# A routed feed-forward kernel: eight widths instead of three for each expert's step, and a last block of at most 64 tokens computed in strips of the TensorE array

## Chip, cores and metric

One core of one Trainium2 chip. The metric is device time in microseconds; the kernel before takes 586.5 us, the median of three runs.

## The reference

An attention layer over 4 batches, 8 heads, 768 positions and 64 dimensions (local window of 96, 8 global keys) gives 3072 token rows of 512. Each token goes to one of 8 experts, the one with the largest logit, and its row is

```
h = np.maximum(np.einsum('ecd,edf->ecf', disp, w1), 0.0)   # 512 -> 1024
y = np.einsum('ecf,efd->ecd', h, w2)                       # 1024 -> 512
out[i] = gate_w[i] * y[expert_idx[i], pos[i]]
```

With the inputs as drawn the eight experts get 455, 416, 361, 397, 367, 410, 395 and 271 tokens.

## The kernel before

The first 240 us compute attention and route the tokens; the change does not touch their code. Then the experts follow one after the other, e = 0 to 7. Their tokens stand in up to four blocks of 128 slots (`T4` = 512 slots). Layer 1 has the weights stationary and the tokens moving: for each of 8 slices f of the hidden layer, 12 matmuls (`layer1`, L844) of w columns into one PSUM bank, `h_ps[f % 2]`, where w is the width of the step. Layer 2 has a block of 128 tokens stationary and 512 columns of w2 moving: 3 matmuls (`layer2`, L852 to L854) for each f and block into the block's bank `y_ps[a]`. Both layers work in float32r on numbers split into a high and a low part, so that a product is three matmuls. `hidden` (L871, L872) makes the two parts of the hidden slice, hh on ScalarE (ACT) and hl on VectorE (DVE); four "pieces" for every second f split the raw weights in the same way (L142 on ACT, L143 on DVE), and `turn` brings in the next expert's tokens (L325 on TensorE, L762, L765).

In step f TensorE runs layer 2 of slice f - 2 for the blocks that every expert has (`SURE`, three of them), then a test of the register `arms[e]` chooses one of three copies of the rest (`widths`): layer 1 with w = 512, 448 or 384, and behind it layer 2 for the fourth block where w is over 384. Only TensorE branches. Slices 6 and 7 of layer 2 run in `last`, behind the next expert's first layer 1, with the fourth block under a test that has no other arm (`with_last`, L830); `finish` (L775) scales a block by the gate and POOL scatters its rows (L777).

The order on TensorE, ACT and DVE in this stage is the order in which the code is written; DMA issues on SP and POOL are placed by the scheduler. Raw weights come in tiles `wr`, eight buffers of 256 KB, two tiles for w1 and two for w2 of a step of two slices; the first three steps are loaded during attention.

Of the kernel before, what the change touches and what calls it, by code (L numbers as in the profile page):

```python
# [20 lines left out]
P = 128  # L21
# [6 lines left out]
def fused(ctx: ExitStack, tc, q, k, v, wg, w1, w2, out, n_global, n_local, cap):  # L28
# [93 lines left out]
    def raw_weights(step, pool, name, bufs, after=()):  # L122
# [662 lines left out]
    STEP, LEAST = 64, 6  # L785
    NV = T4 // STEP - LEAST + 1
    SURE = FIXED - 1
    arm = moe.tile([P, E], I32, name="arm", bufs=1)

    def fill_levels():  # L790
        few = moe.tile([P, E], F32, name="few", bufs=1)
        nc.vector.tensor_scalar(few, run, float(min(cap, T4)), float(STEP - 1), op0=ALU.min, op1=ALU.add)
        nc.vector.tensor_copy(arm, few)
        nc.vector.tensor_scalar(arm, arm, STEP.bit_length() - 1, None, op0=ALU.logical_shift_right)
        nc.vector.tensor_scalar(arm, arm, LEAST, LEAST, op0=ALU.max, op1=ALU.subtract)

    nblk = rt.tile([1, E + 2], I32, name="nblk", bufs=1)
# [15 lines left out]

    arms = {}
# [4 lines left out]
    def widths(e):  # L819

        with tc.If(arms[e] > 0) as more:
            with tc.If(arms[e] > 1) as most:
                yield T4
            with most.Else():
                yield T4 - STEP
        with more.Else():
            yield STEP * LEAST

    def with_last(e):
        with tc.If(arms[e] > 0):  # L830
            yield


    h_ps = [bankB([P, T4]) for _ in range(FP)]
    y_ps = [bankA([P, DM]) for _ in range(FIXED)]

# [28 lines left out]
    def hidden(hs, f, s):  # L865

        if f not in hs:
            hs[f] = (moe.tile([P, T4], F32R, name="hh", bufs=5), moe.tile([P, T4], F32R, name="hl", bufs=5))
        h = h_ps[f % 2]
        hh, hl = hs[f]  # L870
# [35 lines left out]
    for e in range(E):  # L906
# [6 lines left out]
        for f in range(NF):  # L913
# [11 lines left out]
            if f == 4 and e + 1 < E:  # L925
                load_arm(e + 1)
# [125 lines left out]
```

## Time and profile before

| | |
|---|---|
| median of three runs | 586.5 us (584.51 to 587.95) |
| the profiled execution's own time | 591.38 us |
| its span, first to last instruction | 589.2 us |
| TensorE busy | 552.0 us, 94% of the span |
| DVE, ACT, POOL busy | 320.6, 300.6, 107.6 us |
| mean granted TensorE clock | 0.965 of full |

The profile is one execution. Busy time is the time in which at least one matmul was under way, and matmuls overlap, so the time that one costs is the distance from its start to the next one's start. Times in rows count from the span's start.

### The profile page before, as it was taken

To read this page: it belongs to the slowest core of one execution; us is meant where nothing else is said; L and a number is where in the kernel's file an instruction comes from. 1 tells how busy PE (TensorE), PEld (TensorE's weight loads), DVE (VectorE), ACT (ScalarE), POOL (GpSimd) and SP (SyncE) were. 2 spreads that over 40 slices of the span, in tenths; PEclk is the share of its full clock that TensorE was granted. 3 is DMA by queue.
4 is the path that set the end of the run, shared out by engine and by line. 5 is a ranking of instruction groups with operands and counts; after the bars stand their busy time and mean duration, and the time that the engine had idled before them with its cause. 6 is when DMAs were issued, how large, how long until landed. Compare 5 with 4: busy or idle time off the path is not lost.

```text
span 589.2 us, 10890 instructions
## 1 busy us (share of the span) xinstructions
PE 552.0 (94%) x3725; PEld 455.2 (77%) x3725; DVE 320.6 (54%) x1037; ACT 300.6 (51%) x798; POOL 107.6 (18%) x183
## 2 busy tenths in 40 slices
PE   8999987979799999889999999999999999999990
PEld 5677775857677777778888889888898888888970
DVE  6788885858577976624434445343453433533510
ACT  4886775757577785223344354533544434434320
POOL 5103020300103032223122122211222112002011
PEclk9999997979789999799999999999999999999996
DMA  9855554656565422067443455345455453333000
GB/s 214 212 146 146 146 126 153 155 126 160 121 174 130 118 57 82 20 138 264 156 156 126 143 169 179 132 152 159 136 175 169 136 157 123 120 103 129 2 21 24
DMA packets 119262, 78.90 MB, mean 134 GB/s; under 512 B 85837, under 2 KB 102221, under 8 KB 119184
## 3 DMA queue, kind: packets, MB, share of 16 engines
q1 hardware_dynamic: 112608, 63.10, 38.2%
q0 software_dynamic: 5888, 14.71, 8.1%
q8 instruction: 46, 0.75, 0.6%
q14 instruction: 32, 0.26, 0.2%
q10 hardware_dynamic: 688, 0.07, 0.1%
HBM read 60.87 MB, written 14.75 MB: 128 GB/s over the span
## 4 chain that ended last, share of the span: by engine, by line
issue 47%; PE 30%; POOL 10%; DMA 6%; ACT 3%; DVE 1%; POOLq 1%; SPq 0%; DVEq 0%; ACTq 0%
PE bankA L514 8%; POOL out_dram L777 5%; POOL xg L336 5%; DMA nat_v<-in_moe_w_dram 5%; PE bankB L548 4%; PE bankC L458 4%; PE bankC L574 3%; PE bankC L577 3%; PE bankB L555 3%; ACT sc L530 2%; PE bankC L169 2%; PE bankA L190 1%; DMA table<-pay,slot_of 1%; PE bankA L200 1%; PE bankB L74 1%
## 5 line engine op out<-in xcount | busy, mean ns | idle before, releaser
L872 DVE SCALAR_TENSOR_TENSOR hl<-bankB,hh 128x512 fp32r<-128x512 f32 (+1 forms) x67 | 44.6, 668 | 180.6 <-ACT hh L871 180.4
L871 ACT ACTIVATE hh<-bankB 128x512 fp32r<-128x512 f32 (+1 forms) x67 | 38.8, 579 | 172.3 <-PE bankA L854 100.9
L530 ACT ACTIVATE sc<-sc,mx 128x232 f32<-128x232 f32 (+1 forms) x192 | 89.1, 466 | 29.2 <-DVE mx L521 27.8
L844 PE MATMUL bankB<-xh,w1h 128*128 128x448 f32 (+3 forms) x268 | 95.1, 357 | 3.3 <-ACT xh L762 2.1
L844 PE MATMUL bankB<-xh,w1l 128*128 128x448 f32 (+3 forms) x268 | 94.1, 353 | 0.0
L852 PE MATMUL bankA<-w2h,hh 128*128 128x512 f32 x232 | 93.8, 404 | 0.0
L854 PE MATMUL bankA<-w2h,hl 128*128 128x512 f32 x232 | 91.6, 395 | 1.5 <-DVE hl L872 1.5
L853 PE MATMUL bankA<-w2l,hh 128*128 128x512 f32 x232 | 90.8, 391 | 0.0
L521 DVE CUSTOM_DVE_ANT_0 sc<-bankA,bias 128x232 f32<-128x232 f32 (+1 forms) x192 | 64.7, 377 | 17.4 <-PE bankA L514 16.6
L844 PE MATMUL bankB<-xl,w1h 128*128 128x448 f32 (+3 forms) x268 | 61.5, 353 | 0.0
L844 PEld LDWEIGHTS bankB<-xh,w1h 128*128 128x128 f32 x268 | 51.5, 192 | 9.1 <-ACT xh L762 2.7
L844 PEld LDWEIGHTS bankB<-xh,w1l 128*128 128x128 f32 x268 | 51.6, 193 | 4.7
L336 POOL DMA_INDIRECT xg<-xrows,gi x28 | 28.8, 1028 | 135.1 <-PE bankC L325 123.2
L854 PEld LDWEIGHTS bankA<-w2h,hl 128*128 128x128 f32 x232 | 43.6, 188 | 12.2 <-DVE hl L872 2.3
L777 POOL DMA_INDIRECT out_dram<-ysb,tb x30 | 29.6, 986 | 121.0 <-ACT ysb L775 120.1
L844 PEld LDWEIGHTS bankB<-xl,w1h 128*128 128x128 f32 x268 | 48.8, 192 | 2.8
L852 PEld LDWEIGHTS bankA<-w2h,hh 128*128 128x128 f32 x232 | 43.7, 188 | 7.1 <-ACT hh L871 0.4
L853 PEld LDWEIGHTS bankA<-w2l,hh 128*128 128x128 f32 x232 | 43.7, 188 | 7.1
L514 PE MATMUL bankA<-KH,QH 64*128 64x232 f32 (+1 forms) x192 | 41.9, 352 | 6.8 <-ACT QH L459 5.9
L548 PE MATMUL bankB<-ident,sc 128*128 128x128 f32 x192 | 41.1, 297 | 4.3 <-ACT sc L530 4.3
L514 PEld LDWEIGHTS bankA<-KH,QH 64*128 64x128 f32 x192 | 23.9, 191 | 22.0 <-issue 7.9
L577 PE MATMUL bankC<-ptB,nat_v 128*64 128x128 f32 x384 | 38.7, 281 | 0.0
(154 smaller groups left out, 958.8 us busy)
## 6 DMA issues: line engine op xcount, KB each, us to landing
wr<-in_moe_w_dram SPq DMA_DIRECT2D x116, 256.0 KB
nat_q<-in_q_dram SPq DMA_DIRECT2D x24, 256.0 KB
nat_k<-in_k_dram SPq DMA_DIRECT2D x24, 256.0 KB
nat_v<-in_v_dram SPq DMA_DIRECT2D x24, 256.0 KB
xrows<-xr SPq DMA_DIRECT2D x23, 256.0 KB
v<-nat_v SPq DMA_DIRECT2D x20, 192.0 KB
nat_v<-in_moe_w_dram SPq DMA_DIRECT2D x12, 256.0 KB
out_dram<-ysb,tb POOLq DMA_INDIRECT x30, 2.8
```

What stands on the lines that cost most here:

```text
L336: ld = nc.gpsimd.indirect_dma_start(out=xg, out_offset=None, in_=xrows[0:n], in_offset=bass.IndirectOffsetOnAxis(ap=gi.bitcast(U32), axis= ...
L514: m = nc.tensor.matmul(pss[hh][:, gg, :], qq[rows, g, :], win, start=a == 0, stop=a == 2)
L521: nc.vector.tensor_tensor_reduce(out=sc[:, a, 0:w], in0=pss[hh][:, gg, :], in1=bias[:, 2 * g + hh, :], scale=1.0, scalar=3.0e38, op0=ALU.a ...
L530: un["e"] = nc.scalar.activation(sc[:, a, 0:w], sc[:, a, 0:w], AF.Exp, bias=un["mx"][:, a:a + 1], scale=-1.0, accum_out=sm[:, a:a + 1])
L548: un["turned"] = nc.tensor.transpose(pb[:, a, :], un["sc"][:, a, o:o + P], ident)
L577: nc.tensor.matmul(o_ap, d["v"][:, h * D:(h + 1) * D], un["ptB"][:, a, :], start=j == 0, stop=True)
L777: w = nc.gpsimd.indirect_dma_start(out=out, out_offset=bass.IndirectOffsetOnAxis(ap=rows.bitcast(U32)[:, 0:1], axis=0), in_=ysb, in_offset ...
L844: nc.tensor.matmul(h_ps[:, s], ww[:, c, fs], xx[:, c, s], start=n == 0, stop=n == 3 * KC - 1)
L852: nc.tensor.matmul(y, hh[:, t], w2h[:, fi], start=f == 0, stop=False)
L853: nc.tensor.matmul(y, hh[:, t], w2l[:, fi], start=False, stop=False)
L854: nc.tensor.matmul(y, hl[:, t], w2h[:, fi], start=False, stop=f == NF - 1)
L872: nc.vector.scalar_tensor_tensor(hl[:, s], h[:, s], 0.0, hh.bitcast(F32)[:, s], op0=ALU.max, op1=ALU.subtract)
```

## The change

Widths now go in steps of 32 from 288 to 512, eight copies of a step, chosen by a tree of three tests. `SURE` falls to two blocks. In a copy of width w, layer 2 runs first: whole blocks as before (`whole`, a last block counts as whole if it has more than 64 tokens of the width), and a last block of 32 or 64 goes through `beside`: one plain float32 matmul for each f instead of three float32r ones, with 32 or 64 stationary columns, written to a strip of 32 or 64 partitions of the bank `y_ps[3]`; slices f, f + 1, ... go to different strips, so each strip holds a partial sum, and `finish` adds the strips with three DVE operations under a factor `gates` that is the gate or 0. `beside` runs for slices 0 to 3 in step 5 and for slices 4 to 7 in `last`. It needs the hidden slice and w2 unsplit: a third product `hr` of `hidden` (128x256, on ACT) and raw w2 tiles `w2r` (512 KB, seven buffers) that stay until `beside` has read them; `wr` keeps four buffers for w1. The raw w2 of the first three steps is loaded a second time. `take_beside` (15 small DVE operations, once) makes the gates and the row numbers; four small operations join `fill_levels`. In `last` the third and fourth block are now finished first, and slice 7 of the first two blocks comes behind them.

With the counts above the widths before are 512, 448, 384, 448, 384, 448, 448, 384; now 480, 416, 384, 416, 384, 416, 416, 288. Experts 1, 3, 5, 6 have three whole blocks and a strip of 32 instead of four blocks, expert 7 two blocks and a strip of 32 instead of three; experts 0, 2 and 4 keep their blocks and have no strip.

```diff
--- before.py
+++ after.py
...
@@ -128,9 +128,11 @@
             parts = {}
             m = shape[1] // 2
+            if keep and n == "w2":
+                parts["r"] = keep(shape)
             for i in range(2):
                 s = slice(i * m, (i + 1) * m)
-                r = pool.tile([P, m, shape[2]], F32, name=name, bufs=bufs)
+                r = parts["r"][:, s] if "r" in parts else pool.tile([P, m, shape[2]], F32, name=name, bufs=bufs)
                 ld = nc.sync.dma_start(out=r, in_=src[:, s])
...
@@ -773,6 +775,12 @@
     def finish(e, a, rows, y):
         ysb = moe.tile([P, DM], F32, name="ysb", bufs=FIXED)
         nc.scalar.activation(ysb, y, AF.Copy, scale=rows[:, 1:2])
+        if a == FIXED - 1:
+
+            for n, o, m in ((1, 2 * GR, 2 * GR), (0, GR, GR), (0, 3 * GR, GR)):
+                nc.vector.scalar_tensor_tensor(ysb[0:m], y[o:o + m], gates[0:m, e, n:n + 1], ysb[0:m],
+                                               op0=ALU.mult, op1=ALU.add)
...
-    STEP, LEAST = 64, 6
-    NV = T4 // STEP - LEAST + 1
-    SURE = FIXED - 1
+    GR, FINE = 32, 32
+    LOW = 9
+    SURE = GR * LOW // P
...
+    FIRST_ARM = GR * (LOW - 1) // FINE + 1
+    NV = T4 // FINE - FIRST_ARM + 1
...
-    def widths(e):
-
-        with tc.If(arms[e] > 0) as more:
-            with tc.If(arms[e] > 1) as most:
-                yield T4
-            with most.Else():
-                yield T4 - STEP
-        with more.Else():
-            yield STEP * LEAST
-
-    def with_last(e):
-        with tc.If(arms[e] > 0):
-            yield
...
+    def widths(e):
+
+        def among(lo, hi):
+            if hi - lo == 1:
+                yield FINE * (lo + FIRST_ARM)
+                return
+            mid = (lo + hi) // 2
+            with tc.If(arms[e] > mid - 1) as more:
+                yield from among(mid, hi)
+            with more.Else():
+                yield from among(lo, mid)
+        yield from among(0, NV)
...
+    def beside(e, fs, w, hs):
+
+        y = y_ps[FIXED - 1]
+        a, rows = w // P, -(-(w % P) // GR) * GR
+        if rows in (GR, 2 * GR):
+            n = P // rows
+            for f in fs:
+                o = f % n * rows
+                hr = hs[f][2]
+                nc.tensor.matmul(y[o:o + rows], hr[:, (a - SURE) * P:(a - SURE) * P + rows],
+                                 wparts[e * (NF // FP) + f // FP][1]["r"][:, f % FP], start=f < n, stop=f >= NF - n)
+
+    def whole(w):
+
+        return range(SURE, w // P + (w % P > 2 * GR))
...
+    def plain(shape):
+        return moe.tile(shape, F32, name="w2r", bufs=7)
+
     def fetch(step, after=()):
         if step < STEPS and step not in wparts:
-            pieces[step] = raw_weights(step, moe, "wr", 8, after)
+            pieces[step] = raw_weights(step, moe, "wr", 4, after, plain)
...
         nc.scalar.activation(hh[:, s], h[:, s], AF.Relu)
         nc.vector.scalar_tensor_tensor(hl[:, s], h[:, s], 0.0, hh.bitcast(F32)[:, s], op0=ALU.max, op1=ALU.subtract)
+        if s.stop > SURE * P:
+            nc.scalar.activation(hr, h[:, SURE * P:], AF.Relu)
...
+    for step in range(PREFETCH):
+        t = wparts[step][1]["r"] = plain([P, FP, DM])
+        ld = nc.sync.dma_start(out=t, in_=w2[0, step * FP * P:(step + 1) * FP * P, :].rearrange("(f p) d -> p f d", p=P))
+        tc.add_manual_dep(ld.ins, got.ins.name, SYNC)
     fetch(PREFETCH, [got])
...
-            if f > 1:
-                for a in range(SURE):
-                    if e > 0 or f - 2 >= EARLY or a >= FIRST:
-                        second(f - 2, a)
+            h = h_ps[f % 2]
+
+            fs = (f - 2,) if f > 1 else ()
+            for a in range(SURE):
+                second([i for i in fs if e > 0 or i >= EARLY], a)
             part = slice(FIRST * P if e == 0 and f < EARLY else 0, T4)
             for w in widths(e) if e > 0 or f > 1 else ():
-                layer1(e, f, h_ps[f % 2], xh, xl, slice(part.start, w))
-                if f > 1 and w > SURE * P:
-                    second(f - 2, SURE)
+                for a in whole(w):
+                    second(fs, a)
+                if f == 5:
+                    beside(e, range(0, 4), w, hs)
+                layer1(e, f, h, xh, xl, slice(part.start, w))
             hidden(hs, f, part)
             if f == 0 and last is not None:
                 last()
+            if f == 3 and e == 0:
+                to = take_beside(tb)
...
-        def last(e=e, second=second):
+        def last(e=e, second=second, hs=hs):
             for a in range(SURE):
-                for f in (NF - 2, NF - 1):
-                    second(f, a)
+                second((NF - 2,), a)
+            for w in widths(e):
+                beside(e, range(4, NF), w, hs)
+                for a in whole(w):
+                    second((NF - 2, NF - 1), a)
+            rest = [finish(e, a, to[:, e, a - SURE], y_ps[a]) for a in range(SURE, FIXED)]
+            rest[0]()
+            for a in range(SURE):
+                second((NF - 1,), a)
                 finish(e, a, first["early"][:, a] if e == 0 and a < FIRST else tb[:, e, a], y_ps[a])()
-            for _ in with_last(e):
-                for f in (NF - 2, NF - 1):
-                    second(f, SURE)
-            finish(e, SURE, tb[:, e, SURE], y_ps[SURE])()
+            rest[1]()
...
```

On TensorE, step 5 of expert 1 before: the copy for w = 448 has layer 1 and then the fourth block, and a branch ends it (the rows from its last layer 1 group to the next copy; every row is an instruction, x4 four alike, and a plain matmul row holds its weight load).

```order
L844 MATMUL bankB<-xl,w1h 128x448 x4
L852 MATMUL bankA<-w2h,hh 128x512
L853 MATMUL bankA<-w2l,hh 128x512
L854 MATMUL bankA<-w2h,hl 128x512
L822 UNCONDITIONAL_BRANCH
```

And now, the copy for w = 416 in step 5 of expert 3:

```order
L884 MATMUL bankA<-w2h,hh 128x512
L885 MATMUL bankA<-w2l,hh 128x512
L886 MATMUL bankA<-w2h,hl 128x512
L897 MATMUL bankA<-w2r,hr 32x512 [waits DMAHW6_49]
L897 MATMUL bankA<-w2r,hr 32x512 [waits DMAHW7_49]
L897 MATMUL bankA<-w2r,hr 32x512 [waits DMAHW0_49]
L897 MATMUL bankA<-w2r,hr 32x512 [waits DMAHW1_49,Activation_49]
L876 MATMUL bankB<-xh,w1h 128x416
```

The three matmuls of L884 to L886 are the third block, which stood ahead of the tests before; the fourth block's three are gone, four strip matmuls stand between layer 2 and layer 1, and each of the four waits for a load of its own.

On TensorE, the test for the fourth block in `last` before (expert 1; the other experts' are alike):

```order
L830 COMPARE_AND_BRANCH
L852 MATMUL bankA<-w2h,hh 128x512
L853 MATMUL bankA<-w2l,hh 128x512
L854 MATMUL bankA<-w2h,hl 128x512
L852 MATMUL bankA<-w2h,hh 128x512
L853 MATMUL bankA<-w2l,hh 128x512
L854 MATMUL bankA<-w2h,hl 128x512
L830 UNCONDITIONAL_BRANCH
L830 UNCONDITIONAL_BRANCH [waits PE_49]
```

And now the lower copies of the tree that stands there, w = 320 and 288, to the end of the tree and the slice 7 of the first block behind it:

```order
L897 MATMUL bankA<-w2r,hr 64x512 [waits DMAHW2_49]
L897 MATMUL bankA<-w2r,hr 64x512 [waits DMAHW3_49,Activation_49]
L863 UNCONDITIONAL_BRANCH
L897 MATMUL bankA<-w2r,hr 32x512 [waits DMAHW7_49]
L897 MATMUL bankA<-w2r,hr 32x512
L897 MATMUL bankA<-w2r,hr 32x512 [waits DMAHW2_49]
L897 MATMUL bankA<-w2r,hr 32x512 [waits DMAHW3_49,Activation_49]
L863 UNCONDITIONAL_BRANCH
L884 MATMUL bankA<-w2h,hh 128x512
L885 MATMUL bankA<-w2l,hh 128x512
L886 MATMUL bankA<-w2h,hl 128x512 [waits DVE_49]
```

The path that skips the fourth block had a wait of TensorE for its own matmuls (PE_49); every path of the new tree holds matmuls, and no such wait stands in it.

On SP, the first loads of the expert stage before (tbf is an early copy of the table of slots, tb the table, wr raw weights of step 3 on):

```order
L174 DMA xrows<-xr_last 128x512 [waits DMAHW4_49,DVE_49]
L134 DMA wr<-in_moe_w_dram 128x2x256 [waits DMAHW1_49,DMAHW2_49,DMAHW0_49,DMAHW5_49,DMASW2_49,DMAHW6_49,PE_49,DMAHW7_49,Activation_49,Pool_49]
L738 DMA tb<-table 128x4x2 [waits DMASW7_49,DMASW3_49,DMASW0_49]
L738 DMA tb<-table 128x4x2 x4
L738 DMA tb<-table 128x4x2 [waits DMAHW3_49]
L738 DMA tb<-table 128x4x2 [waits DMAHW4_49]
L738 DMA tb<-table 128x4x2 [waits DMAHW5_49]
L134 DMA wr<-in_moe_w_dram 128x2x256 [waits DMAHW6_49]
L134 DMA wr<-in_moe_w_dram 128x512 [waits DMAHW7_49]
```

And now:

```order
L959 DMA w2r<-in_moe_w_dram 128x2x512 [waits DMAHW1_49,DMAHW2_49,DMAHW0_49,DMAHW5_49,DMASW2_49,DMAHW6_49,PE_49,DMAHW7_49,Activation_49,Pool_49]
L740 DMA tb<-table 128x4x2 [waits DMASW7_49,DMASW3_49,DMASW0_49]
L740 DMA tb<-table 128x4x2 x4
L740 DMA tb<-table 128x4x2 [waits DMAHW3_49]
L740 DMA tb<-table 128x4x2 [waits DMAHW4_49]
L740 DMA tb<-table 128x4x2 [waits DMAHW5_49]
L959 DMA w2r<-in_moe_w_dram 128x2x512 [waits DMAHW6_49]
L959 DMA w2r<-in_moe_w_dram 128x2x512 [waits DMAHW7_49]
L136 DMA wr<-in_moe_w_dram 128x2x256 [waits DMAHW0_49]
```

The three second loads of raw w2, 512 KB each, have moved in ahead of the first w1 tile of step 3.

## Rows read from the trace of the kernel before

**Rows 1.** The page's busy times (us, share of the span, instructions), granted TensorE clock in 40 slices of the span (tenths of full), and the queue that brings TensorE's instructions (packets, MB, share of 16 engines' time).

```profile
span 589.2 us, 10890 instructions
PE 552.0 (94%) x3725; PEld 455.2 (77%) x3725; DVE 320.6 (54%) x1037; ACT 300.6 (51%) x798; POOL 107.6 (18%) x183
...
PEclk9999997979789999799999999999999999999996
...
q8 instruction: 46, 0.75, 0.6%
```

**Rows 2.** Busy time of each engine in stretches of the expert stage (stretch, its length, busy us and instructions of TensorE matmuls, weight loads, DVE, ACT, POOL, then granted clock, DMA share, GB/s).

```profile
260.00:270.00 10.00, 8.54 (x39) 6.64 (x38) 3.98 (x8) 3.14 (x6) 5.17 (x5) 1.00 0.90 297
...
300.00:340.00 40.00, 40.00 (x196) 34.81 (x195) 18.69 (x37) 16.98 (x31) 6.07 (x6) 1.00 0.45 143
```

**Rows 3.** All waits of TensorE's matmuls from 260 us on (who, for whom: us in total, times, longest).

```profile
PE bankA L854 <- DVE hl L872: 1.5, 1, 1.5
PE bankB L844 <- PEq L830: 1.2, 2, 0.6
```

**Rows 4.** Groups of instructions by shape, 258 to 575 us (x count | busy us, mean ns of one | idle before and its releaser).

```profile
L844 PE MATMUL bankB<-xh,w1h 128*128 128x448 f32 x128 | 46.9, 366 | 1.2 <-PEq L830 1.2
...
L872 DVE SCALAR_TENSOR_TENSOR hl<-bankB,hh 128x512 fp32r<-128x512 f32 x61 | 42.2, 692 | 177.3 <-ACT hh L871 177.3
...
L871 ACT ACTIVATE hh<-bankB 128x512 fp32r<-128x512 f32 x61 | 36.5, 598 | 160.2 <-PE bankA L854 98.5 <-PE bankB L844 61.7
L142 ACT CAST w1h<-wr 128x512 fp32r<-128x512 f32 x58 | 32.9, 617 | 0.7 <-DMA wr<-in_moe_w_dram 0.7
...
L844 PE MATMUL bankB<-xh,w1h 128*128 128x384 f32 x96 | 32.4, 338 | 0.0
...
L775 ACT ACTIVATE ysb<-bankA,tb 128x512 f32<-128x512 f32 x30 | 20.3, 688 | 19.8 <-PE bankA L854 19.8
...
L871 ACT ACTIVATE hh<-bankB 128x256 fp32r<-128x256 f32 x2 | 0.8, 384 | 3.4 <-PE bankA L854 2.4 <-PE bankB L844 1.0
```

**Rows 5.** TensorE's matmuls in order of time (start us, us, instruction): the first of twelve layer 1 matmuls of 512, then 448 columns, the layer 2 matmul behind each twelve, and the next layer 1 twenty-four layer 2 matmuls later.

```profile
285.89 0.39 PE L844 MATMUL bankB<-xh,w1h 128*128 128x512 f32 x1
...
288.68 0.40 PE L852 MATMUL bankA<-w2h,hh 128*128 128x512 f32 x1
...
289.38 0.37 PE L844 MATMUL bankB<-xh,w1h 128*128 128x448 f32 x1
...
291.80 0.40 PE L852 MATMUL bankA<-w2h,hh 128*128 128x512 f32 x1
...
297.32 0.36 PE L844 MATMUL bankB<-xh,w1h 128*128 128x448 f32 x1
```

**Rows 6.** The same view, twelve layer 1 matmuls of 256 columns and of 384 columns, first and behind the last.

```profile
256.61 0.28 PE L844 MATMUL bankB<-xh,w1h 128*128 128x256 f32 x1
...
258.02 0.40 PE L852 MATMUL bankA<-w2h,hh 128*128 128x512 f32 x1
...
344.40 0.34 PE L844 MATMUL bankB<-xh,w1h 128*128 128x384 f32 x1
...
346.49 0.40 PE L852 MATMUL bankA<-w2h,hh 128*128 128x512 f32 x1
```

**Rows 7.** The same view in the attention stage. L190 is the router's product: four float32 matmuls of 32 stationary columns and 384 moving ones, each to its own 32 partitions; a float32 product leaves two records, so x8. L458 and L548 use all 128 columns. L577 has 64 stationary columns, two products beside each other in two halves, x4 for two products; a group like it (L574) stands between the two shown.

```profile
67.23 0.60 PE L458 MATMUL bankC<-ident,nat_q 128*128 128x128 f32 x4
67.76 0.85 PE L190 MATMUL bankA<-xt,wg_sb 128*32 128x384 f32 x8
68.54 0.33 PE L548 MATMUL bankB<-ident,sc 128*128 128x128 f32 x1
...
71.36 0.66 PE L458 MATMUL bankC<-ident,nat_k 128*128 128x128 f32 x4
71.85 0.60 PE L548 MATMUL bankB<-ident,sc 128*128 128x128 f32 x4
...
236.48 0.39 PE L577 MATMUL bankC<-ptB,nat_v 128*64 128x128 f32 x4
...
236.93 0.39 PE L577 MATMUL bankC<-ptB,nat_v 128*64 128x128 f32 x4
```

**Rows 8.** TensorE in order of time where expert 2 skips its fourth block.

```profile
375.45 0.40 PE L854 MATMUL bankA<-w2h,hl 128*128 128x512 f32 x1
376.43 0.48 PE L844 MATMUL bankB<-xh,w1h 128*128 128x448 f32 x1 [0.58 <-PEq L830]
```

**Rows 9.** The branches on L821 on TensorE's sequencer (duration ns min/median/max, first and last start): all of them, and the one between 340.5 and 341.5 us, which chooses the copy whose first matmul starts at 344.40 us.

```profile
L821 PEldq COMPARE_BRANCH  x62: 65/70/340, 257.7 to 563.3; - x62
...
L821 PEldq COMPARE_BRANCH  x1: 207/207/207, 340.8 to 340.8; - x1
```

**Rows 10.** ACT in expert 0, in order of time (idle before and its releaser in brackets).

```profile
262.59 0.62 ACT L142 CAST w1h<-wr 128x512 fp32r<-128x512 f32 x1 [0.71 <-DMA wr<-in_moe_w_dram]
266.92 0.60 ACT L871 ACTIVATE hh<-bankB 128x512 fp32r<-128x512 f32 x1 [3.70 <-PE bankA L854]
```

**Rows 11.** The end: ACT and POOL in order of time from the last layer 1 on.

```profile
569.22 0.60 ACT L871 ACTIVATE hh<-bankB 128x512 fp32r<-128x512 f32 x1 [3.57 <-PE bankB L844]
573.89 1.26 ACT L775 ACTIVATE ysb<-bankA,tb 128x512 f32<-128x512 f32 x2 [0.69 <-PE bankA L854]
...
576.13 0.97 POOL L777 DMA_INDIRECT out_dram<-ysb,tb  x1 [0.30 <-issue]
```

More of the change, by code (lines that the diff above doesn't have):

```diff
@@ L120, in fused, with raw_weights @@
     wparts = {}
-    def raw_weights(step, pool, name, bufs, after=()):
+    def raw_weights(step, pool, name, bufs, after=(), keep=None):
         e, fp = divmod(step, NF // FP)
@@ L781, in finish @@
         return scatter
-    STEP, LEAST = 64, 6
-    NV = T4 // STEP - LEAST + 1
-    SURE = FIXED - 1
+    GR, FINE = 32, 32
+    LOW = 9
+    SURE = GR * LOW // P
+    level = moe.tile([P, E], I32, name="level", bufs=1)
+    FIRST_ARM = GR * (LOW - 1) // FINE + 1
+    NV = T4 // FINE - FIRST_ARM + 1
     arm = moe.tile([P, E], I32, name="arm", bufs=1)
+    nblk = rt.tile([1, E + 2], I32, name="nblk", bufs=1)
     def fill_levels():
         few = moe.tile([P, E], F32, name="few", bufs=1)
[L792 to L797, printed above, removed]
+        for t, step, low in ((arm, FINE, FIRST_ARM), (level, GR, LOW)):
+            nc.vector.tensor_scalar(few, run, float(min(cap, T4)), float(step - 1), op0=ALU.min, op1=ALU.add)
+            nc.vector.tensor_copy(t, few)
+            nc.vector.tensor_scalar(t, t, step.bit_length() - 1, None, op0=ALU.logical_shift_right)
+            nc.vector.tensor_scalar(t, t, low, low, op0=ALU.max, op1=ALU.subtract)
     def count_blocks():
@@ L812, in count_blocks, with take_beside @@
         nc.vector.tensor_scalar(nblk, nblk, 7, None, op0=ALU.logical_shift_right)
+    gates = moe.tile([P, E, 2], F32, name="gates", bufs=1)
+    def take_beside(tb):
+        swap = moe.tile([P, E], F32, name="swap", bufs=1)
+        nc.vector.tensor_scalar(swap, level, 2.0, None, op0=ALU.is_lt)
+        to = moe.tile([P, E, 2, 2], F32, name="to", bufs=1)
+        for c, t in ((0, I32), (1, F32)):
+            d = moe.tile([P, E], t, name="d", bufs=2)
+            i, o = tb.bitcast(t)[:, :, :, c], to.bitcast(t)[:, :, :, c]
+            nc.vector.tensor_tensor(d, i[:, :, SURE], i[:, :, SURE + 1], op=ALU.subtract)
+            nc.vector.tensor_tensor(d, d, swap, op=ALU.mult)
+            nc.vector.tensor_tensor(o[:, :, 0], i[:, :, SURE], d, op=ALU.subtract)
+            nc.vector.tensor_tensor(o[:, :, 1], i[:, :, SURE + 1], d, op=ALU.add)
+        bits = moe.tile([P, E], I32, name="bits", bufs=1)
+        for n, m in ((0, P // GR - 1), (1, P // GR // 2)):
+            nc.vector.tensor_scalar(bits, level, m, None, op0=ALU.bitwise_and)
+            nc.vector.tensor_scalar(gates[:, :, n], bits, 0.0, None, op0=ALU.is_equal)
+            nc.vector.tensor_tensor(gates[:, :, n], gates[:, :, n], to[:, :, 1, 1], op=ALU.mult)
+        return to
     arms = {}
@@ L867, in hidden @@
         if f not in hs:
-            hs[f] = (moe.tile([P, T4], F32R, name="hh", bufs=5), moe.tile([P, T4], F32R, name="hl", bufs=5))
+            hs[f] = (moe.tile([P, T4], F32R, name="hh", bufs=5), moe.tile([P, T4], F32R, name="hl", bufs=5),
+                     moe.tile([P, T4 - SURE * P], F32, name="hr", bufs=7))
         h = h_ps[f % 2]
-        hh, hl = hs[f]
+        hh, hl, hr = hs[f]
         nc.scalar.activation(hh[:, s], h[:, s], AF.Relu)
         nc.vector.scalar_tensor_tensor(hl[:, s], h[:, s], 0.0, hh.bitcast(F32)[:, s], op0=ALU.max, op1=ALU.subtract)
+        if s.stop > SURE * P:
+            nc.scalar.activation(hr, h[:, SURE * P:], AF.Relu)
     EARLY = 3
@@ L897, in fused @@
                 xs[2](FIRST + a, y_ps[FIRST + a])
-            layer2(0, f - 2, a, y_ps[a], *hs0[f - 2])
+            layer2(0, f - 2, a, y_ps[a], *hs0[f - 2][0:2])
     for f in range(2):
@@ L908, in fused, with second @@
         hs = hs0 if e == 0 else {}
-        def second(f, a, e=e, hs=hs):
-            layer2(e, f, a, y_ps[a], *hs[f])
+        def second(fs, a, e=e, hs=hs):
+            for f in fs:
+                layer2(e, f, a, y_ps[a], *hs[f][0:2])
         for f in range(NF):
```

## Prediction

> **What bounds the kernel now.** I read the windows of the expert stage first, because the change touches nothing earlier. In the stretch 300 to 340 us TensorE's matmuls are busy 40.00 of 40.00 us at a granted clock of 1.00, while DVE has 18.7, ACT 17.0 and the DMA queues 45% [rows 2]. Next come the waits: from 260 us to the end all of TensorE's waits together are one of 1.5 us for DVE's hl and two of about 0.6 us for its own sequencer at L830 [rows 3]. So in these 300 us nothing but the number and the width of matmuls sets the time, until the tail, where the last expert's blocks go through ACT and POOL one behind the other [rows 11]. A matmul taken away from this stage is worth its spacing in the timeline, and a matmul added costs it. That spacing comes from rows 5 and 6.
>
> **A. Layer 2 matmuls removed.** Twenty-four layer 2 matmuls in a row take 297.32 - 291.80 = 5.52 us, 0.230 us each [rows 5]. Experts 1, 3, 5 and 6 lose their fourth block and expert 7 its third: 5 experts x 8 slices x 3 = 120 matmuls, -27.6 us.
>
> **B. Narrower layer 1.** Twelve matmuls take 2.79 us at 512 columns, 2.42 at 448 [rows 5], 2.09 at 384 and 1.41 at 256 [rows 6], so 0.2325, 0.2017, 0.1742 and 0.1175 us each. From 448 to 416 (experts 1, 3, 5, 6: 4 x 8 x 12 = 384 matmuls, of which the row of one of the three products counts 128 [rows 4]) half the step between the two rows is saved, 0.0138 us each: -5.3. From 384 to 288 (expert 7, 96 matmuls) 288 lies a quarter of the way from 256 to 384, at 0.1317, so 0.0425 each: -4.1. From 512 to 480 (expert 0, the six steps that choose a copy, 72 matmuls) 0.0154 each: -1.1. Together -10.5. The least that the narrower copies can save is nothing, if 416 costs what 448 does; but the four widths lie almost on one line, so I take the line.
>
> **C. The skipped test.** When experts 2 and 4 skip the fourth block, TensorE stands 0.58 to 0.6 us for its own earlier matmuls [rows 3, 8]. In the new tree every path has matmuls and no such wait: -1.2.
>
> **D. The strips.** Ten groups (two each for experts 1, 3, 5, 6, 7) of four float32 matmuls with 32 stationary and 512 moving columns. The nearest row is the router's product: four of them with 384 columns, eight records, in 68.54 - 67.76 = 0.78 us [rows 7], the change back to whole-array matmuls included. Eight records that took turns could hardly stand in 0.78 us: a single float32 product is two records, and if the four ran one behind the other a record would have 0.10 us for 384 columns, where twelve float32r matmuls of that width take 0.174 each. So the four strips run side by side, in two rounds of 0.39 us; scaled to 512 columns a group is 1.04 us. The change into strips is the difference between four L458 ahead of the router (0.53) and four ahead of whole-array work (0.49): 0.04 us. I take 1.1 a group: +11.0. The bounds: 0.78 (no growth with columns) gives +7.8; all four in turn 4 x 1.04 + 0.1 = 4.3 gives +43. I take the lower part because the row is the same form but for the columns. One thing differs: here three or four of the strips carry a DMA wait of their own. Those loads landed steps ago, so the waits hold nothing; they only could keep the four from being overlapped.
>
> The Trainium skill, page "TensorEngine Tiling (Array Packing)", section "Key Properties", states that changing the tiling mode drains TensorE. The trace shows little of it: 0.04 us on the way in. At the drain of rows 8 on both sides of each group it would be 2 x 0.58 x 10 = 11.6 us more, and D would be +22.6.
>
> **E. The tail.** After the last layer 1 (its end is T = 569.2, where hh begins) the last scatter ended at 577.10, T + 7.9 [rows 11]. The chain will be hh 0.6, hl 0.69, hr 0.38 [rows 4] and hand-overs, about T + 2.0; TensorE fills this with slice 6 of two blocks; then the strips, T + 3.1; ysb of the third and fourth block, 2 x 0.69; three dependent DVE additions, for which the nearest row is hl, at 0.69 each, 2.1 us; 0.9 us from the last ysb to the scatter, as before (575.15 to 576.13) [rows 11]; the scatter 0.97; with some 0.6 for the hand-overs that no row shows, T + 9.1. A and D already count -1.38 + 1.1 = -0.3 inside this tail, so the correction is 1.2 + 0.3 = +1.5. It could be 0, if the additions run at half the price on 32 and 64 partitions.
>
> **F. The rest, +0.5.** The third product hr costs ACT 0.38 us (the 128x256 row) and makes it wait for hl of the same bank, 0.7. ACT's work in a step of a whole expert is then hh 0.6, hl's 0.7, hr 0.4, two casts of 0.62 and turning work of about 0.5: 3.4 us, under TensorE's step of nine layer 2 and twelve layer 1 matmuls (9 x 0.23 + 12 x 0.188 = 4.3 us). Without that cover hr would cost 62 x 0.38 = 24 us. Only expert 7 is near the edge: its step falls to 6 x 0.23 + 12 x 0.132 = 2.96 us. I leave 0.5 for it. The 15 and 4 small DVE operations lie under DVE's idle half [rows 2]. The three second loads, 1.57 MB at the 297 GB/s of that stretch [rows 2], put the first w1 tile back by 5.3 us, from about 262.6 to 268. ACT now waits 0.7 for that tile and then idles 3.7 before the next hh [rows 10], and the tile's slices are needed two steps later; without that slack the loads cost up to 5.3.
>
> Eight copies with three tests stand where three copies with two stood. A test takes TensorE's sequencer 65 to 70 ns, and the sequencer is 3.6 us ahead of the array (the test at 340.8 chooses the copy that starts at 344.40) [rows 9]; a third test and a longer jump are hidden as long as that lead holds. Cost taken: 0.
>
> **Sum.** -27.6 - 10.5 - 1.2 + 11.0 + 1.5 + 0.5 = -26.3 us against the profiled execution's 591.4: 565.1. That execution is 0.8% above the median of 586.5; the same 4.4% off the median is 560.5 us.
>
> **The rivals.**
> *Strips half side by side.* If the two rounds of one product stay next to each other, each second round overlaps only with the next strip's first: five rounds of 0.52 and 0.1, 2.7 us a group, +16 to the sum: 576.5. For it: four waits between them; against it: 0.78 us in rows 7.
> *Strips with drains.* By the price above, 572.
> *The strips in turn.* 4.3 us a group, 32 more than taken: 592.5, slower by 1%. This is decided at 3.7 us a group, where the ten eat the other terms' 37. Rows 7 speak against it.
> *The tree shows.* If each of the 70 trees holds the array as the skipped test does now, 0.58 us [rows 8], that is +41: 601, slower. The point from which it decides is 26.3 / 70 = 0.375 us a tree. A fetch of TensorE's instructions takes (0.6% of 16 x 589.2) / 46 = 1.2 us of a queue [rows 1]; TensorE's program doubles, and one such fetch in each jump would use a third of the 3.6 us lead, three of them all of it. The 62 present tests show no wait of this kind [rows 3]. The Trainium skill, "Runtime: NRT & Kernel Launch", "Instruction fetch mechanics", states that a taken branch to a target outside the two pages at hand must wait for a fetch; no row here shows one.
> *Early loads not hidden.* +5.3: 566.
> *The change gives nothing.* ACT's third product frees each PSUM bank later and TensorE waits for it in each step, 24 us: 584.5. ACT's 3.4 against 4.3 us speaks against it.
>
> **How the numbers follow.** Full gain 0.62 (its own range 554 to 566: D from 7.8, E from 0, half of B's doubt); half side by side 0.12; drains 0.06; early loads 0.06; in turn 0.05; trees 0.06; nothing 0.03. The range goes to the half-overlapped strips: 554 to 577. The three runs spread 0.6%, so 0.5%, 2.9 us, is about what can be told. Faster: 0.62 + 0.12 + 0.06 + 0.06 and a little of the last, 0.87; same 0.04 (nothing, and a part of "in turn"); slower 0.09.
>
> **What will show it.** TensorE's matmul count on the path falls by 120 and rises by 80 strip records. A group's first strip to the next matmul: 1.1 us, against 2.7 or 4.3. Layer 1 of 416 columns: twelve in 2.26 us. The windows stay at 40.00 of 40.00 busy; if waits for the sequencer appear at the trees, the tree rival is right; waits for hr or for w2r point to ACT or the loads. The end lies 9 us behind the last layer 1. The prediction is wrong if a strip group is over 2 us, or if TensorE stands at the head of the copies.

## The result, and the profile after

The changed kernel takes 569.0 us (median, 565.5 to 570.5) against 585.7, a ratio of 0.970 (95% interval 0.964 to 0.976): 17 us faster, where 26 were forecast. In a second comparison it gave 572.9 us, 0.977 (0.971 to 0.983); two of its six executions there were longer at a lower granted clock, which the median counts and the ratio leaves out. The forecast of 560.5 lies below both intervals; its range, 554 to 577, holds both.

The page of the changed kernel has these lines beside [rows 1] (span, busy times, granted clock, TensorE's and the other engines' instruction loads):

```profile
span 568.8 us, 11038 instructions
...
PE 527.6 (93%) x3685; PEld 427.6 (75%) x3685; DVE 344.6 (61%) x1080; ACT 322.0 (57%) x862; POOL 107.8 (19%) x183
...
PEclk9899997999889999899999999999999999999995
...
q8 instruction: 90, 1.47, 1.2%
```

TensorE's count went from 3725 to 3685: 120 matmuls out and 80 strip records in, as forecast. The instruction queue went from 46 packets and 0.75 MB to 90 and 1.47.

The windows beside [rows 2] (length, busy us and instructions of TensorE matmuls, weight loads, DVE, ACT, POOL, clock, DMA share, GB/s):

```profile
260.00:270.00 10.00, 8.00 (x38) 6.42 (x37) 7.33 (x24) 5.64 (x11) 4.33 (x4) 1.00 1.04 373
270.00:280.00 10.00, 8.22 (x39) 6.62 (x38) 2.92 (x5) 2.50 (x5) 1.23 (x1) 1.00 0.85 293
...
300.00:340.00 40.00, 40.00 (x211) 34.34 (x210) 22.77 (x43) 21.80 (x43) 8.02 (x8) 1.00 0.53 163
340.00:380.00 40.00, 38.79 (x198) 34.62 (x197) 22.12 (x35) 21.98 (x45) 8.02 (x8) 1.00 0.53 167
```

and all waits of its matmuls from 255 to 570 us (who, for whom: us, times, longest), beside [rows 3]:

```profile
PE bankA L884 <- issue: 4.1, 4, 2.0
PE bankA L886 <- DVE hl L924: 2.0, 1, 2.0
PE bankC L327 <- issue: 1.8, 1, 1.8
PE bankB L876 <- issue: 0.8, 1, 0.8
PE bankA L897 <- issue: 0.5, 1, 0.5
```

The wait for hl was there before (1.5 us). The others are new. "issue" means that the array waited for nothing that the profile shows of another engine; its own sequencer had not sent the matmul yet. The sequencer's branches stand just ahead of most of these waits. First all branch records of the trees, then those between 264 and 270 us (duration in ns, min/median/max, first and last start):

```profile
L863 PEldq COMPARE_BRANCH  x271: 65/208/5942, 251.3 to 548.1; - x136
...
L863 PEldq COMPARE_BRANCH  x4: 65/2354/5942, 264.0 to 269.1; - x4
```

The longest branch of a step was 340 ns before [rows 9] and is 5.9 us now. In order of time on TensorE, at one of these places:

```profile
266.61 0.40 PE L886 MATMUL bankA<-w2h,hl 128*128 128x512 f32 x1
269.00 0.50 PE L884 MATMUL bankA<-w2h,hh 128*128 128x512 f32 x1 [2.00 <-issue]
```

A branch that began at 264.31 took 4.64 us, to 268.95; the first matmul behind it started at 269.00. From here "branch time" is the sum of the durations of all TensorE's branch records from about 250 us on, and a "stand" is a matmul of the expert stage that starts later than the median distance for its kind while the array waits for the sequencer. Branch time was 29.6 us before and is 119.4 now (in each kernel 3 to 4 us of it are one branch at the end, which holds up no matmul); stands add up to 10 us, in expert 0 (2.3 and 1.9), in experts 2 and 4 (1.5, 1.1, 0.4, 0.6, 0.9) and in expert 7 (1.3 in three places). The rows of waits above give 7.2 us of it, the time in which no matmul counts as busy; the rest is late starts under the modelled end of the matmul ahead. One stand, 1.1 us in expert 4, has no long branch ahead of it: the branches that start between 400 and 404 us take at most 0.29 us, and the sequencer was late with the third matmul of a copy:

```profile
L863 PEldq COMPARE_BRANCH  x4: 65/142/293, 399.9 to 403.9; - x4
...
403.40 0.44 PE L876 MATMUL bankB<-xh,w1h 128*128 128x384 f32 x1 [0.85 <-issue]
```

The pair of profiles must be compared within the stage: the first layer 1 began at 241.74 us in the execution of before and at 236.43 in that of after, both at half the granted clock, which lasted to 248.0 us and to 239.8, and the change touches nothing ahead of it. From the first layer 1 of expert 1 to the last hh, before took 569.22 - 289.38 = 279.8 us [rows 5, 11], after 547.50 - 287.29 = 260.2: 19.6 us less.

```profile
287.29 0.35 PE L876 MATMUL bankB<-xh,w1h 128*128 128x416 f32 x1
...
547.50 0.60 ACT L923 ACTIVATE hh<-bankB 128x512 fp32r<-128x512 f32 x1 [1.25 <-PE bankB L876]
```

### The profile page after: what moved, and what is told of

Same layout as the page of the kernel before. It is cut to its first block, busy times and chain, and to the rows that moved or that the text cites. A ratio compares the mean times of both kernels' runs of the same rounds, so it can differ in the third digit from the quotient of the medians.

```text
span 568.8 us, 11038 instructions
## 1 busy us (share of the span) xinstructions
PE 527.6 (93%) x3685; PEld 427.6 (75%) x3685; DVE 344.6 (61%) x1080; ACT 322.0 (57%) x862; POOL 107.8 (19%) x183
## 3 DMA queue, kind: packets, MB, share of 16 engines
q8 instruction: 90, 1.47, 1.2%
## 4 chain that ended last, share of the span: by engine, by line
issue 48%; PE 29%; POOL 9%; DMA 7%; ACT 3%; DVE 2%; POOLq 0%; SPq 0%; DVEq 0%; ACTq 0%
PE bankA L516 8%; DMA nat_v<-in_moe_w_dram 5%; POOL xg L338 4%; PE bankB L550 4%; PE bankC L460 4%; PE bankC L576 3%; PE bankC L579 3%; POOL out_dram L785 3%; PE bankB L557 3%; ACT sc L532 2%; PE bankC L171 1%; DMA xg<-xrows,gi 1%; PE bankA L202 1%; DMA table<-pay,slot_of 1%; PE bankA L192 1%
## 5 line engine op out<-in xcount | busy, mean ns | idle before, releaser
L876 PE MATMUL bankB<-xh,w1h 128*128 128x416 f32 (+5 forms) x268 | 91.3, 345 | 2.7 <-ACT xh L764 1.5
L876 PE MATMUL bankB<-xh,w1l 128*128 128x416 f32 (+5 forms) x268 | 89.7, 340 | 0.0
L923 ACT ACTIVATE hh<-bankB 128x512 fp32r<-128x512 f32 (+1 forms) x67 | 38.8, 579 | 89.0 <-PE bankB L876 88.8
L884 PE MATMUL bankA<-w2h,hh 128*128 128x512 f32 x192 | 79.4, 413 | 4.2 <-issue 4.1
L886 PE MATMUL bankA<-w2h,hl 128*128 128x512 f32 x192 | 76.1, 396 | 2.0 <-DVE hl L924 2.0
L885 PE MATMUL bankA<-w2l,hh 128*128 128x512 f32 x192 | 75.7, 394 | 0.0
L876 PE MATMUL bankB<-xl,w1h 128*128 128x416 f32 (+5 forms) x268 | 57.3, 336 | 0.0
L926 ACT ACTIVATE hr<-bankB 128x256 f32<-128x256 f32 x64 | 24.6, 384 | 54.9 <-DVE hl L924 54.9
L145 DVE TENSOR_TENSOR w1l<-wr,w1h 128x512 fp32r<-128x512 f32 x58 | 37.6, 688 | 29.8 <-ACT w1h L144 29.8
L145 DVE TENSOR_TENSOR w2l<-w2r,w2h 128x512 fp32r<-128x512 f32 x58 | 37.4, 687 | 19.1 <-ACT w2h L144 18.2
L884 PEld LDWEIGHTS bankA<-w2h,hh 128*128 128x128 f32 x192 | 36.1, 188 | 15.8 <-issue 10.4
L886 PEld LDWEIGHTS bankA<-w2h,hl 128*128 128x128 f32 x192 | 36.1, 188 | 11.3 <-DVE hl L924 2.4
```

The source lines that it names most:

```text
L145: nc.vector.tensor_tensor(parts["l"][:, s], r, parts["h"].bitcast(F32)[:, s], op=ALU.subtract)
L876: nc.tensor.matmul(h_ps[:, s], ww[:, c, fs], xx[:, c, s], start=n == 0, stop=n == 3 * KC - 1)
L884: nc.tensor.matmul(y, hh[:, t], w2h[:, fi], start=f == 0, stop=False)
L885: nc.tensor.matmul(y, hh[:, t], w2l[:, fi], start=False, stop=False)
L886: nc.tensor.matmul(y, hl[:, t], w2h[:, fi], start=False, stop=f == NF - 1)
```

## The experiments

Every ratio is to the kernel before on the same chip. Two theories stand against each other first. *Program length*: eight copies make TensorE's program nearly twice as long (21,900 instructions instead of 11,200), and its sequencer has to wait in the branches until the next part of it is brought in. *The new work*: strips, the third product, or the second loads of w2.

**Eight copies around the old work.** In the kernel before, STEP and LEAST become 32 and 9, and the tests become the tree of the changed kernel.

```diff
+        def among(lo, hi):
+            if hi - lo == 1:
+                yield max(384, -(-STEP * (lo + LEAST) // 64) * 64)
...
```

> The kernel before, with its old widths, blocks and loads, but each of its 62 steps goes through a tree of three tests and eight copies (equal widths stand in several copies). Theory: longer trees alone make TensorE's sequencer stand in its branches (119 us of branch time after, 29.6 before), so the branches show 1 to 5 us in some steps here too and the stage gets 5 to 9 us longer: 591 to 595 us against 585.7, with branch time of 80 us or more. Rival: the trees cost nothing, and the missing gain comes from the third product or the strips: 585 to 587 us, branch time about 45 us.

Measured: 589.4 us, ratio 1.003 (0.999 to 1.007); branch time 64.7 us; no stand in a tree but 0.3 us in expert 0, and 0.8 more at the two skipped fourth blocks. Neither theory had it all: the branch time rose to twice that of before with 19,900 instructions, and it stayed hidden, so the time can't be told from that of before. The wait at the two skipped blocks (L833) is the first row of its waits:

```profile
PE bankB L847 <- PEq L833: 1.9, 2, 1.1
```

**The same with a program as long as the changed kernel's.** The third block's layer 2 moves from ahead of the tree into every copy.

```diff
-                for a in range(SURE):
+                for a in range(SURE - 1):
...
+                if f > 1:
+                    second(f - 2, SURE - 1)
                 layer1(e, f, h_ps[f % 2], xh, xl, slice(part.start, w))
```

> The kernel before again in trees of eight copies, and now the third block's layer 2 stands in every copy too: the same matmuls are executed as before, but TensorE's program is as long as that of the changed kernel (21,900 instructions; the eight-copy run had 19,900, the kernel before 11,200). Theory: the sequencer's stands follow from how much program must be brought in per step; branch time rises from 65 us toward the changed kernel's 119 (over 90), and stands of 1 us show at the heads of copies, 2 to 6 us in all: 588 to 592. Rival: the stands belong to the new work (strips, third product, w2r loads, shorter steps); branch time stays near 65 us, no stands, 586 to 588.

Measured: 587.1 us, 1.001 (0.996 to 1.005); branch time 94.5 us. Its waits, beside the same 1.9 us for the skipped blocks:

```profile
PE bankC L325 <- issue: 1.4, 1, 1.4
PE bankB L847 <- ACT hh L874: 0.8, 1, 0.8
```

The last row, at 362.30 us, is put down to hh, but a branch of 3.48 us that began at 357.93 and two short ones end just ahead of it. So a longer program alone, with no strip, no third product and no second load, brings the long branches back. But with the old, longer steps of 4.2 to 5.6 us the array covers most of them: some 3 us of stands besides the skipped blocks, and a time that can't be told from that of before. The theory was right on the branch time and too high on its price here.

**Without the second loads.** The loop of three loads is taken out, and with it expert 0's strips (its 455 tokens use none).

```diff
-    for step in range(PREFETCH):
-        t = wparts[step][1]["r"] = plain([P, FP, DM])
...
-        if rows in (GR, 2 * GR):
+        if e > 0 and rows in (GR, 2 * GR):
```

> The changed kernel without the three second loads of raw w2 (expert 0 has no strip code in its copies; with these counts it uses none). Theory: the two longest stands in the trees (2.0 and 1.8 us, at 267 to 275 us) fall together with DMA queues busy 0.85 to 1.04 in the first 20 us of the stage, since the loads of TensorE's instructions share them; without the 1.57 MB both shrink to under 0.7 us each and the time falls by 2 to 4 us: 565 to 567. Rival: a jump's length alone sets the stand; both stay, no change (569).

Measured: 566.6 us, 0.965 (0.961 to 0.970); branch time 113.7. The interval overlaps that of the changed kernel (0.964 to 0.976), so the gain of about 2 us isn't shown by the time. In the trace the two stands of expert 0 became one of 1.1 us, but one of 2.6 us stood ahead of expert 7's strips.

**The second loads later.** Each is issued in steps 1 to 3 of expert 0.

```diff
+            if e == 0 and 1 <= f <= PREFETCH:
+                t = wparts[f - 1][1]["r"] = plain([P, FP, DM])
...
```

> The changed kernel with the three second loads issued in steps 1 to 3 of expert 0, behind the first tiles of step 3, instead of ahead of them. Theory: the same bytes in a quieter stretch; the first expert gains most of what it gains without them, 1 to 3 us: 566 to 568. If the stands only move to where the loads now are, 569.

Measured: 572.7 us (565.5 to 577.2), 0.971 (0.964 to 0.978), branch time 122.5: no gain, where 1 to 3 us were expected. The two stands of expert 0 are there again (1.2 and 1.7 us).

**Four copies.** FINE is 64, and a strip has w % 128 columns.

```diff
-    GR, FINE = 32, 32
+    GR, FINE = 32, 64
...
-        a, rows = w // P, -(-(w % P) // GR) * GR
+        a, rows = w // P, w % P
```

> The changed kernel with four copies in steps of 64 slots (512, 448, 384, 320), and strips of 64. Theory: trees half as long have hardly a stand in their branches, -7 to -10 us; the narrower widths are given back: layer 1 of 448 instead of 416 (384 x 0.0138 = 5.3), 320 instead of 288 (96 x 0.014 = 1.4), 512 instead of 480 (1.1), and strips of 64 in two rounds instead of one (10 x 1.0), +17.8; sum +8 to +11: 577 to 580. Rival, trees cost nothing: +17.8, 587.

Measured: 576.4 us, 0.983 (0.977 to 0.989). Branch time 38.2 us and no stand in a tree, read in an execution of 587.6 us with a granted clock of 1.00 in the expert stage. The median time is about what the sum for that work without stands says: 26.3 - 17.8 = 8.5 us less than before, 10 measured. Strips of 64 took 1.87 us a group.

**Six copies.** The widths 352 and 480, which change nothing in layer 2, are computed as 384 and 512.

```diff
+        ends = (0, 1, 3, 4, 5, 7)
...
-                yield FINE * (lo + FIRST_ARM)
+                yield FINE * (ends[lo] + FIRST_ARM)
...
-            with tc.If(arms[e] > mid - 1) as more:
+            with tc.If(arms[e] > ends[mid - 1]) as more:
...
-        yield from among(0, NV)
+        yield from among(0, len(ends))
```

> The changed kernel with six copies: 352 is computed as 384 and 480 as 512, the two widths that change nothing in layer 2. TensorE's program has 17,500 instructions instead of 21,900. Only expert 0 of these inputs is given a wider layer 1, +1.1 us. Theory of program length: branch time falls from 119 to about 70 us, stands from 10 to 2 to 4 us, so 562 to 564 us against 569. Rival, the DMA load alone makes the stands: 569 to 570.

Measured: 557.5 us (556.3 to 561.0), 0.953 (0.949 to 0.958): 27 us faster than before and, by the two ratios of the changed kernel (0.970 and 0.977), 10 to 14 faster than that, though expert 0's layer 1 is wider. The theory had expected 562 to 564 us and a branch time of 70. Its instruction queue, all its waits from 255 us on, its tests, the stretch where expert 0 stood, a later one, and the first layer 1 of expert 1 and last hh:

```profile
q8 instruction: 73, 1.20, 0.9%
...
PE bankA L887 <- DVE hl L925: 1.9, 1, 1.9
...
L864 PEldq COMPARE_BRANCH  x226: 65/176/1641, 249.3 to 534.6; - x113
...
260.00:270.00 10.00, 10.00 (x49) 8.11 (x48) 7.10 (x25) 5.58 (x11) 2.46 (x3) 1.00 1.03 374
...
340.00:380.00 40.00, 40.00 (x208) 36.23 (x208) 22.52 (x35) 22.74 (x45) 8.65 (x9) 1.00 0.52 165
...
281.61 0.35 PE L877 MATMUL bankB<-xh,w1h 128*128 128x416 f32 x1
...
535.69 0.60 ACT L924 ACTIVATE hh<-bankB 128x512 fp32r<-128x512 f32 x1 [1.25 <-PE bankB L877]
```

All waits for issue are gone; branch time is 47.8 us. The DMA queues are as busy as in the changed kernel at 260 to 270 us (1.03, 374 GB/s), and TensorE runs 10.00 of 10.00 us there: the second loads make no stand by themselves. Experts 1 to 7 take 535.69 - 281.61 = 254.1 us by the measure above, 25.8 less than before. The forecast for that stretch, with its parts of A to D and F, was 26.4.

**Six copies' work in eight copies.** 384 and 512 stand twice in the tree; what is executed stays.

```diff
-        ends = (0, 1, 3, 4, 5, 7)
+        ends = (0, 1, 3, 3, 4, 5, 7, 7)
...
-            with tc.If(arms[e] > ends[mid - 1]) as more:
+            with tc.If(arms[e] > mid - 1) as more:
```

> The six-copy kernel with its program padded to the length of the changed kernel: eight copies again, where the two extra ones repeat 384 and 512, so TensorE executes the matmuls of the six-copy run but its program is 21,908 instructions long, as the changed kernel's. Theory of program length: branch time back from 48 to about 115 us, stands of 6 to 10 us, 566 to 569 us. Rival, the six-copy run was faster for another reason (widths, the chip): 557 to 559.

Measured: 568.4 us (566.1 to 578.2), 0.969 (0.963 to 0.974); branch time 124.7. Its waits show what came back:

```profile
PE bankA L885 <- issue: 2.1, 4, 1.1
PE bankA L887 <- DVE hl L925: 2.1, 1, 2.1
PE bankC L327 <- issue: 1.3, 1, 1.3
PE bankB L877 <- issue: 0.9, 1, 0.9
PE bankA L898 <- issue: 0.5, 1, 0.5
```

Same matmuls, same loads, 4,400 more instructions that are never executed: 0.969 against 0.953, some 9 us. Six copies without strips for expert 0 (below), timed on the same chip beside this kernel, took 559.2 us. So copies that never run cost the time; that much is settled. What is not told apart is by what: two widths also take one test more, so that 271 branch records stand against 226 (45 more at the median of 0.21 us make 9 of the 77 us of branch time added), and the jumps are longer.

**Short jumps, same length.** Layer 2 of the second to fourth block goes ahead of the big tree, in three copies.

```diff
+                with tc.If(arms[e] > 5) as four:
+                    for a in range(SURE - 1, FIXED):
+                        second(fs, a)
+                with four.Else():
+                    with tc.If(arms[e] > 1) as three:
...
-                for a in whole(w):
+                for a in () if byself else whole(w):
```

> The changed kernel with eight copies of layer 1 alone, and layer 2 of the second to fourth block in a tree of three copies ahead of it. The program is hardly shorter (21,300 instructions), but the jump over the upper half of the big tree falls from about 140 to 105 instructions, below the 127 of the eight-copy run on the old work, whose first jumps took 0.4 us. Theory of program length: branch time stays at 100 to 120 us, 568 to 570. Rival, the length of the one jump: first jumps take 0.4 us instead of 1.4 to 4, stands vanish but in expert 0, 563 to 565.

Measured: 561.5 us (561.0 to 564.9), 0.961 (0.957 to 0.966). Branch time is 114.6 us, as the theory of length says, but of that 22 us belong to the new tests, and the big tree's own fell to 88.8 us from 115.6; the time is below what either theory gave. The branches of the big tree between 336 and 360 us (expert 2), in this kernel and then in the changed one:

```profile
L863 PEldq COMPARE_BRANCH  x24: 65/176/1007, 335.9 to 358.3; - x24
```

```profile
L863 PEldq COMPARE_BRANCH  x18: 65/176/4096, 336.7 to 357.0; - x18
```

The waits are shorter one by one and more of them lie under the array's work; the stand of 2.1 us in expert 0, one of 0.9 at 435 us and smaller ones in expert 7 remain. So the same program length goes with less waiting and fewer stands when the jumps are shorter: both seem to have a say, and how much each has isn't shown. Why a given jump waits 0.4 or 4 us isn't settled here.

**Without the strips.** beside does nothing, whole takes every started block, and the gates of the strips are 0.

```diff
-        if rows in (GR, 2 * GR):
+        if False:
...
-        return range(SURE, w // P + (w % P > 2 * GR))
+        return range(SURE, -(-w // P))
```

> The changed kernel without the strips: a last block of any size is a whole block, all else stays (eight copies, third product, second loads). By the sum: 120 layer 2 matmuls come back (+27.6 us), ten groups of strips go (-11.9 by the spacing in the trace of the changed kernel), and the longer steps hide more of the sequencer's stands (0 to -5): 580 to 585 us. Rival, strips save little because their waits and changes of mode cost as much as the block: 569 to 574.

Measured: 579.2 us, 0.991 (0.987 to 0.994), just under the 580 to 585 expected. Against the changed kernel's 0.970 and 0.977 the strips are worth 1.3 to 2.0% of the time, 8 to 12 us, in the kernel with eight copies: 15.7 by the spacings, less the stands that longer steps cover (some 5 us of stands are left in its trace, against 10). The rest of the change, with the stands, is worth 1%.

**Six copies, no strips for expert 0.** Expert 0 takes any last block whole, which needs no second loads; their loop is taken out.

```diff
+        nc.vector.tensor_scalar(level[:, 0:1], level[:, 0:1], 7, None, op0=ALU.max)
...
-        return range(SURE, w // P + (w % P > 2 * GR))
+        return range(SURE, w // P + (w % P > (2 * GR if e > 0 else 0)))
```

> Six copies, and expert 0 takes a last block of any size as a whole block, so that no strips and no second loads of raw w2 are needed for it (one more small DVE operation). In the six-copy run no stand is left in expert 0, so by the theory of program length the second loads now cost nothing: 556 to 558, the same as six copies. Rival, the loads still delay something in the first 20 us of the stage: 554 to 555.

Measured: 559.2 us, 0.953 (0.948 to 0.957), the same ratio as six copies. With the short program the 1.57 MB cost nothing that the time shows.

**The changed kernel once more**, beside the last two.

> The changed kernel once more beside the two others: 567 to 570 us, with 5 or more stands in its trees, most of them where the first test is false (experts 2, 4 and 7) or in expert 0.

Measured: 572.9 us (566.9 to 578.4), over the 567 to 570 expected; five stands are over 0.3 us, in experts 0, 2, 4 (two) and 7, where they were expected. In its profiled execution (566.9 us) the first stand of expert 0 cost more than itself. TensorE's rows at it, and the windows from 260 us on:

```profile
263.70 0.40 PE L886 MATMUL bankA<-w2h,hl 128*128 128x512 f32 x1
266.38 0.56 PE L884 MATMUL bankA<-w2h,hh 128*128 128x512 f32 x1 [2.28 <-issue]
266.74 0.63 PE L885 MATMUL bankA<-w2l,hh 128*128 128x512 f32 x1
267.17 0.63 PE L886 MATMUL bankA<-w2h,hl 128*128 128x512 f32 x1
```

```profile
260.00:264.00 4.00, 4.00 (x20) 3.13 (x19) 3.73 (x19) 2.44 (x6) 1.93 (x2) 1.00 1.05 388
264.00:267.00 3.00, 0.72 (x3) 0.55 (x3) 2.04 (x5) 1.57 (x4) 0.00 (x0) 0.95 1.03 383
267.00:272.00 5.00, 5.00 (x17) 3.93 (x16) 1.24 (x3) 0.32 (x1) 0.00 (x0) 0.69 1.03 361
```

## Why the prediction came out as it did

**What bounds the kernel.** Right: TensorE still sets the stage, and six copies run 40.00 of 40.00 us.

**A and B.** Right. The spacings of the changed kernel's timeline are as interpolated: twelve layer 1 matmuls of 416 columns in 2.25 us (2.26 forecast), twelve of 288 in 1.59 (1.58). The first lines of each twelve and the line behind it:

```profile
295.18 0.35 PE L876 MATMUL bankB<-xh,w1h 128*128 128x416 f32 x1
...
297.43 0.39 PE L884 MATMUL bankA<-w2h,hh 128*128 128x512 f32 x1
...
542.65 0.30 PE L876 MATMUL bankB<-xh,w1h 128*128 128x288 f32 x1
...
544.24 0.40 PE L884 MATMUL bankA<-w2h,hh 128*128 128x512 f32 x1
```

**C.** Right: no wait for the sequencer at a skipped block is left.

**D.** Right. One group of strips, from the matmul ahead to the second one behind:

```profile
313.17 0.40 PE L886 MATMUL bankA<-w2h,hl 128*128 128x512 f32 x1
313.50 1.07 PE L897 MATMUL bankA<-w2r,hr 128*32 128x512 f32 x8
314.49 0.46 PE L876 MATMUL bankB<-xh,w1h 128*128 128x416 f32 x1
314.79 0.35 PE L876 MATMUL bankB<-xh,w1l 128*128 128x416 f32 x1
```

The four run side by side, 0.99 us, with 0.10 us on the way in and 0.11 on the way out: 1.20 a group against 1.1, +1 us over the ten. The rivals "half side by side" (2.7), "with drains" (2.3) and "in turn" (4.3) fall with this row. By the Trainium skill's rule of a drain at each change of mode ("TensorEngine Tiling (Array Packing)", "Key Properties") the change would show; it shows as 0.1 us each way, not as the 0.58 us of [rows 8].

**E.** Nearly right. The last hh begins at 547.50, the last scatter ends at 555.17 + 0.97 = 556.14, 8.6 us later (9.1 forecast, 7.9 before [rows 11]). The three additions took 0.75 us each, no less for 32 and 64 partitions, but POOL's four scatters of 1.28 us apiece are what ends last.

```profile
551.67 2.32 DVE L781 SCALAR_TENSOR_TENSOR ysb<-bankA,gates,ysb 64x512 f32<-64x512 f32 x3 [2.85 <-ACT ysb L777]
...
555.17 0.97 POOL L785 DMA_INDIRECT out_dram<-ysb,to  x1 [0.30 <-issue]
```

**F.** Right in the main. No matmul waits for hr or for w2r, and the third product is hidden, in expert 7 too. The one wait for hl, in expert 0, grew by 0.5 us. Whether the second loads cost up to 2 us with eight copies isn't shown by the time of the kernel without them.

**The step that failed: "Cost taken: 0" for the trees.** It rested on one lead of 3.6 us, read at one place of the old program [rows 9], and on the tests of L821 alone. Branches of the new program take up to 5.9 us, more than that lead. The lead itself looks like a number of queued matmuls: at 57 of the 62 tests of the old program, 16 or 17 matmuls start between the test and its copy, whatever time they take (3.2 to 4.0 us). Narrower matmuls then cover less: in expert 7, whose twelve layer 1 matmuls take 1.59 us, branches of 1.6 to 2.5 us were enough. The trace of before held a warning that [rows 9] left out, TensorE's branch past the code for experts of more than 512 tokens, which stands behind the last matmul:

```profile
L979 PEldq COMPARE_BRANCH  x1: 4050/4050/4050, 574.5 to 574.5; - x1
```

It takes 4.05 us, more than the lead, while ACT, DVE, POOL and SP take 50 to 72 ns for the same branch; in the changed kernel it takes 3.83 us. So where the prediction says of a jump that has to wait that "no row here shows one", the trace did show one, in the short program. The stands took 10 us, 0.14 us a tree on the mean, against the 0.375 at which the rival "the tree shows" would have undone the whole gain. That rival had the right place and too high a price; the likeliest case had the rest right. By the prediction's own sign, "if TensorE stands at the head of the copies", it was wrong here. That the range holds 569.0 us is luck: the likeliest case's own range ended at 566, and it was drawn out to 577 for strips that overlap by half, which did not come. Sum with the measured sizes: -26.3 + 1.0 (D) + 10 (stands) + 0.5 (hl's wait) - 0.5 (E) = -15.3 us; the medians give -16.7.

The Trainium skill, "Runtime: NRT & Kernel Launch", "Instruction fetch mechanics", names such a stall for a taken branch whose target isn't in the pages at hand, and was set aside because no row named there showed one. The runs here bear it out in kind: nearly all the waits lie in the branches, and branch time is 29.6 us with 46 packets of instructions, 47.8 with 73 and 119.4 with 90. That the sequencer waits for a fetch in them is argued from this; no record shows the fetch itself. Its blocks of 16 KiB agree with the queue's packets (1.47 MB / 90 = 16.3 KB).

## What to carry to other kernels

A copy of code under a test costs nothing where it isn't executed, until the sequencer must wait to be brought past it: count the instructions of all copies, compare them with the program before, and merge copies that save little (two widths of eight saved 1.1 us here and cost some 9). A lead read from a trace covers a branch only as long as the matmuls that it consists of are as many and as wide as in that trace. When a sum of matmul spacings is right to 1 us and the time is not, look at the engine's own branches before looking at other engines, and at all of them: the longest one of the old program was not at the line that the change touches.

## What the runs showed of the hardware

In the steps of the experts TensorE's branch records last 65 to 340 ns in a program of 11,200 TensorE instructions and up to 5.9 us in one of 21,900; with 17,500, 3 of 226 last over 0.5 us and the longest 1.6. The one branch past the code for larger experts takes 3.4 to 4.1 us in every kernel here. Four float32 matmuls with 32 stationary and 512 moving columns, each to its own 32 partitions, take 0.99 us together, and four with 64 take 1.87.

A stand of the sequencer can also cost granted clock. Behind the 2.28 us without work in the second run of the changed kernel, seen above, the next matmuls stood 0.43 us apart instead of 0.23: the granted clock was at its lower level, 1.2 GHz, for the first three of the next five us (their mean is 0.69), and some 1.6 us went on top of the stand. In the first run a stand of 2.00 us left the clock at 1.00, while in the kernel without strips one of 1.99 us, to 262.64 us, was followed by the lower level:

```profile
263.00:266.00 3.00, 3.00 (x10) 2.43 (x9) 1.86 (x3) 1.04 (x2) 1.35 (x1) 0.50 1.06 389
```

So the stands alone don't say when the clock falls.
